# Attention ahead of two mixtures of experts: loading keys and queries by token instead of by token pair

## The chip, the cores and the metric

The kernel runs on one core of a Trainium2 chip. The metric is the device time of one execution in microseconds, the median of three runs. A profile of one further execution gives the trace that is read here. Engine names are those of the profile: PE (matrix products and transposes through the array), PEld (its weight loads), DVE (vector engine), ACT (scalar engine), POOL, and SP, whose queue issues most DMAs.

## What is computed

Block-local attention over 4 batches, 8 heads, 576 tokens and a head size of 64, then a mixture of experts with top-1 routing (8 experts, capacity 576), then a dense mixture with a Sinkhorn gate. The change touches the attention and the order of expert 0's loads only.

```
q_c, k_c, v_c = (a.reshape(B, H, nc, 64, D) for a in (q, k, v))
scores = scale * q_c @ k_c^T                 # within chunks of 64 tokens
attn = exp(scores - max); attn /= attn.sum(-1) + 1e-9
x = (attn @ v_c) -> [2304 tokens, 512]
x = moe(x, w_gate, w1, w2, capacity)         # top-1: relu(x @ w1[e]) @ w2[e], times the gate
out = moe2(x, w_gate, w1, w2)                # every expert, weights from 8 Sinkhorn rounds
```

## The kernel before

Attention goes over 18 tiles of 128 tokens (two chunks of 64), as a pipeline written out by hand. A loop over steps n runs the list `order`: each entry is a stage function and its lag, and stage f works on tile n minus lag. Every engine executes its share in exactly that order. A tile passes these stages: `st_tr` turns queries and keys on PE into a bank of PSUM and copies them out; `st_scores` multiplies them (per head pair, the keys as a block-diagonal matrix `kbd` of two heads); `st_max` (DVE) takes the maximum and subtracts; `st_dtr` turns the difference on PE; `st_exp` (ACT) writes eT; `st_pv` multiplies with `vbd`, a block-diagonal form of v; `st_x1` (DVE) normalises; `st_norm`, `st_scale`, `st_hi`, `st_lo` scale the row, split it into two half-precision parts and store it to `xs_d`; `st_xtr`, `st_xcopy` and `st_logits` turn x and multiply it with the first gate. Every three tiles `route` adds small DVE, PE and POOL work.

Keys and queries come in tiles of 256 tokens (`load_qk`, L433): a partition holds two consecutive tokens, so each packet of the DMA is 512 bytes. `st_tr` alternates: on an even step it turns the eight head pieces of a k tile, on an odd one the eight of a q tile. Since a turned piece holds two tokens on its 128 partitions, each of its two banks is copied out by two copies of 64 partitions, which put the tokens back in order (L458 for k, L461 for q): four half copies a step. For the first two 256-token tiles DVE does the copies of one bank; the rest are ACT's. The buffers are 2 for k, 4 for q, one for the copied q (`qT`), two for `kbd`. `load_v` (L443) issues four DMAs of 64 partitions a tile, 256-byte packets.

The turned pieces, the differences and x share three PSUM banks in turn (`in_turn("p", ...)`). Expert 0's weights are loaded, measured (`w_stat`, a sum of squares on ACT, L168), scaled and split (`w_split`: a high part on ACT, L239, a low part on DVE, L242) in quarters, at steps that the `plan` list fixes: the first matrix ("a") is loaded from step 4 on, the second ("b") from step 9. The steps from 18 on only drain the pipeline; at step 21 the first tokens of expert 0 are gathered and turned (`turn_into`), and `first_product` follows.

Of the kernel before, what the change touches and what calls it, by code (L numbers as in the profile page):

```python
# [11 lines left out]
F32 = mybir.dt.float32  # L12
# [18 lines left out]
def kernel(ctx, tc, q, k, v, w_gate, w1, w2, capacity, w2_gate, w21, w22, out):  # L31
    nc = tc.nc
    B, H, S, D = q.shape
    N, DM = out.shape
    E, _, F = w1.shape
    CH = 64
    NT = N // 128
    PR = H // 2
# [57 lines left out]
    ident = const.tile([128, 128], F32, name="ident")  # L96
# [204 lines left out]

    NS = N // 256
    runs = []
    for i in range(NS):
        r, done = [], 0
        while done < 256:
            b, s = divmod(i * 256 + done, S)
            n = min(256 - done, S - s)
            r.append((done // 2, n // 2, b, s))
            done += n  # L310
        runs.append(r)
# [57 lines left out]
    with ExitStack() as actx:  # L369
# [10 lines left out]
        nc.gpsimd.memset(warm, 0.0)  # L380
        kbd = [bd.tile([128, PR, 4, 128], F32, name=f"kbd{j}") for j in range(2)]
        for j in range(2):
# [42 lines left out]
        T = [dict() for _ in range(NT)]  # L425
        ST = [dict() for _ in range(NS)]
        GT = [dict() for _ in range(NG)]

        def load_qk(i):
            for nm, src in (("k", k), ("q", q)):  # L430
                t = io.tile([128, H, 2, D], F32, tag=nm, name=f"{nm}{i}", bufs=4 if nm == "q" else 2)
                for off, n, b, s in runs[i]:
                    nc.sync.dma_start(out=t[off:off + n].rearrange("p h t d -> p h (t d)"),  # L433
                                      in_=src[b, :, s:s + 2 * n, :].rearrange("h (s t) d -> s h (t d)", t=2))
                ST[i][nm] = t

# [8 lines left out]
        def st_tr(i):  # L445
            i, nm = i // 2, "kq"[i % 2]
            src = ST[i].pop(nm)
            t = ST[i][nm + "T"] = kbd[i % 2] if nm == "k" else at.tile([128, PR, 256], F32, tag="qT", name="qT", bufs=1)
            for h2 in range(2):
                p = in_turn("p", [128, PR, 128], F32, "p_t")  # L450
                for pr in range(PR):
                    nc.tensor.transpose(p[:, pr, :], src[:, 2 * pr + h2, :, :].rearrange("p t d -> p (t d)"), ident)
                hs = slice(64 * h2, 64 * h2 + 64)
                copy = nc.vector.tensor_copy if i < 2 and h2 == 0 else nc.scalar.copy
                for a in range(2):
                    pa = p[64 * a:64 * a + 64, :, :]
                    if nm == "k":
                        copy(out=t[hs, :, :, hs].rearrange("p r c (s t) -> p t r c s", t=2)[:, a],  # L458
                                       in_=pa.rearrange("p r (c s) -> p r c s", c=4))
                    else:  # L460
                        copy(out=t[hs].rearrange("p r (s t) -> p t r s", t=2)[:, a], in_=pa)  # L461

        def st_scores(i):
            qT, kT = ST[i // 2]["qT"], ST[i // 2]["kT"]
            p = ps_s.tile([128, PR, 128], F32, tag="s", name="p_s")
            for pr in range(PR):
                for c in range(2):
                    cc = 2 * (i % 2) + c
                    nc.tensor.matmul(p[64 * c:64 * c + 64, pr, :], lhsT=qT[:, pr, 64 * cc:64 * cc + 64],
                                     rhs=kT[:, pr, cc, :])  # L470
            T[i]["p"] = p.rearrange("p r (a s) -> p (r a) s", a=2)
# [77 lines left out]
        def st_xcopy(i):  # L549
            xT = T[i]["xT"] = at.tile([128, KD, 128], F32, tag="xT", name="xT")  # L550
            (nc.vector.tensor_copy if i % 3 == 1 or (i < 6 and i % 3 == 2) else nc.scalar.copy)(out=xT, in_=T[i].pop("xp"))

# [132 lines left out]

        load_qk(0)
        nc.scalar.activation(out=warm, in_=warm, func=AF.Exp)
        load_v(0)
        load_qk(1)
        nc.gpsimd.dma_start(out=g1, in_=w_gate.rearrange("(k p) e -> p k e", p=128))  # L690
# [14 lines left out]
        for h in range(2):  # L705
            plan(NT + 1, lambda h=h: w_load(1, "a", h))
        for nm, ld, st, sc, sp in (("a", 4, 6, 9, (11, 12, 13, 14)), ("b", 9, 11, 14, (18, 19, 20, 20))):
            for h in range(4):
# [883 lines left out]
```

## Time and profile before

| | us |
|---|---|
| median of 3 runs | 1741.5 (1738.76 to 1743.41) |
| profiled execution | 1743.53 |
| its span | 1741.8 |
| PE busy | 1691.9 |
| DVE busy | 1199.1 |
| ACT busy | 953.5 |
| POOL busy | 726.7 |

The span counts from the first to the last instruction of the profiled execution. A busy time is the sum over the instructions of an engine; for PE the ends of matrix products are modelled, so a busy PE isn't PE at its peak. The attention stage is the first 115 us or so of the span; the stretches and the order of time inside them tell more of it than the totals.

### The profile page before, as it was taken

The numbers are of one execution on the slowest core, as the hardware profiler recorded it, in microseconds if no ns is written. First come the engines' busy times: TensorE is split into PE (matmuls) and PEld (weight loads), VectorE is DVE, ScalarE is ACT, GpSimd is POOL, SyncE is SP. The second block draws the span as 40 slices with busy tenths as digits, with TensorE's granted clock in tenths as the row PEclk, the third lists the DMA queues.
The fourth block names the chain that finished last, engine by engine and source line by source line (L and its number), as shares of the span: only waits on it lengthen the run. The fifth ranks groups of instructions, "written<-read, shape, count | busy, mean of one in ns | idle before, by whom it ended". The sixth has DMA issues, their size and how long they took to land.

```text
span 1741.8 us, 33426 instructions
## 1 busy us (share of the span) xinstructions
PE 1691.9 (97%) x13203; PEld 1224.7 (70%) x13203; DVE 1199.1 (69%) x2336; ACT 953.5 (55%) x1805; POOL 726.7 (42%) x765
## 2 busy tenths in 40 slices
PE   8889999989999999999999999999999999999997
PEld 6775666655555577777777777777777767777776
DVE  7886857755578666776676767677766686677554
ACT  6976756754445554665455545455644665354431
POOL 2335644622023243553445434453534543453443
PEclk9999999999999999999999999999999999999999
DMA  9948878745242413242233224323323241323201
GB/s 227 248 142 243 228 182 195 198 113 143 82 155 94 144 53 134 65 176 85 92 129 131 87 98 148 107 86 113 130 89 133 65 174 47 131 66 126 91 34 49
DMA packets 140344, 219.17 MB, mean 126 GB/s; under 512 B 62304, under 2 KB 80832, under 8 KB 140160
## 3 DMA queue, kind: packets, MB, share of 16 engines
q1 hardware_dynamic: 134768, 199.46, 36.6%
q0 software_dynamic: 5392, 17.26, 3.6%
q8 instruction: 115, 1.88, 0.5%
q14 instruction: 69, 0.57, 0.2%
HBM read 167.56 MB, written 41.91 MB: 120 GB/s over the span
## 4 chain that ended last, share of the span: by engine, by line
PE 69%; DVE 5%; ACT 2%; issue 1%; POOL 1%; POOLq 0%; ACTq 0%; DVEq 0%
PE p_m L1283 36%; PE p_m L1379 28%; PE p_m L1427 5%; DVE wall L297 3%; DVE acc L1350 1%; ACT wall L296 1%; PE p_m L1171 0%; ACT eh L1288 0%; POOL out_dram L1361 0%; DVE el L1291 0%; ACT tq L1323 0%; DVE tq L1298 0%; POOL el L1295 0%; DVE tq L1301 0%; DVE wall L255 0%
## 5 line engine op out<-in xcount | busy, mean ns | idle before, releaser
L1283 PE MATMUL p_m<-x,wall 128*128 128x384 f16 x4032 | 667.7, 326 | 4.9 <-ACT tq L1323 4.1
L1295 POOL TENSOR_TENSOR el<-tq,eh 128x384 f16<-128x384 f32 x336 | 346.8, 1060 | 568.6 <-ACT eh L1288 567.9
L1379 PE MATMUL p_m<-wall,eh 128*128 128x256 f16 x3528 | 580.3, 273 | 0.0
L1283 PEld LDWEIGHTS <-wall 128*128 128x128 f16 x4032 | 394.3, 98 | 262.6 <-issue 8.3
L1379 PE MATMUL p_m<-wall,el 128*128 128x256 f16 x1764 | 480.8, 273 | 0.0
L1288 ACT ACTIVATE eh<-tq 128x384 f16<-128x384 f32 x540 | 274.1, 522 | 190.2 <-DVE tq L1301 101.4
L1379 PEld LDWEIGHTS <-eh 128*128 128x128 f16 x3528 | 344.3, 98 | 44.4
L1350 DVE SCALAR_TENSOR_TENSOR acc<-p_m,cf,acc 128x256 f32<-128x256 f32 (+1 forms) x378 | 175.6, 521 | 130.7 <-PE p_m L1379 130.7
L1298 DVE TENSOR_TENSOR tq<-p_m,tq 128x384 f32<-128x384 f32 x288 | 158.4, 556 | 127.9 <-PE p_m L1283 126.8
L1379 PEld LDWEIGHTS <-el 128*128 128x128 f16 x1764 | 172.6, 98 | 19.9
L1291 DVE SCALAR_TENSOR_TENSOR el<-tq,eh 128x384 f16<-128x384 f32 x204 | 175.2, 860 | 10.0 <-ACT eh L1288 8.6
L1301 DVE SCALAR_TENSOR_TENSOR tq<-tq 128x384 f32<-128x384 f32 x252 | 133.1, 553 | 2.8
L353 PEld LDWEIGHTS <-wall 128*128 128x128 f16 x1344 | 107.3, 98 | 19.3 <-issue 7.2
L1323 ACT COPY tq<-p_m 128x384 f32<-128x384 f32 x96 | 45.6, 475 | 112.4 <-PE p_m L1283 109.9
L1427 PE MATMUL p_m<-wall,eh 128*128 128x512 f16 x288 | 85.6, 379 | 0.0
L275 POOL TENSOR_TENSOR tq<-stb 128x256 f32<-128x256 f32 x56 | 48.9, 873 | 81.9 <-DVE wsumsq L184 59.0
L1336 ACT ACTIVATE tq<-tq 128x384 f32<-128x384 f32 x84 | 43.9, 522 | 69.9 <-DVE tq L1298 69.9
L353 PE MATMUL p_p<-xT,wall 128*128 128x256 f16 x672 | 75.6, 272 | 3.7 <-DMA rk_d<-rkt 1.5
L296 ACT ACTIVATE wall<-stb,wsb 128x256 f16<-128x256 f32 (+1 forms) x56 | 31.3, 606 | 87.0 <-DMA wb_d<-wall 61.5
L275 POOL TENSOR_TENSOR tq<-sta 128x256 f32<-128x256 f32 x56 | 45.0, 804 | 72.8 <-DVE wall L297 43.3
L247 POOL TENSOR_SCALAR stb<-stb,wsb 128x1024 f32<-128x1024 f32 x16 | 53.6, 3350 | 52.0 <-DVE tq L1298 45.1
L297 DVE SCALAR_TENSOR_TENSOR wall<-stb,wsb,wall 128x256 f16<-128x256 f32 (+1 forms) x56 | 38.1, 690 | 50.9 <-ACT wall L296 48.1
(283 smaller groups left out, 2115.5 us busy)
## 6 DMA issues: line engine op xcount, KB each, us to landing
x<-xt_d SPq DMA_DIRECT2D x147, 384.0 KB
wb_d<-wall SPq DMA_DIRECT2D x20, 896.0 KB
wall<-wb_d SPq DMA_DIRECT2D x20, 896.0 KB
sta<-in_moe_w_dram SPq DMA_DIRECT2D x32, 512.0 KB
stb<-in_moe_w_dram SPq DMA_DIRECT2D x32, 512.0 KB
sta<-in_moe_w_dram SPq DMA_DIRECT2D x16, 1024.0 KB
stb<-in_moe_w_dram SPq DMA_DIRECT2D x16, 1024.0 KB
xt_d<-x SPq DMA_DIRECT2D x21, 384.0 KB
```

The lines of the kernel that those rows point to most:

```text
L275: nc.gpsimd.tensor_tensor(out=at(o), in0=at(u), in1=at(v), op=op)
L297: nc.vector.scalar_tensor_tensor(out=o[:, cs, 1], in0=src, scalar=m.s, in1=o[:, cs, 0], op0=ALU.mult, op1=ALU.subtract)
L353: nc.tensor.matmul(p[:, f4, :], lhsT=w[:, kk, f * 128:(f + 1) * 128], rhs=xT[:, lo + kk, 0:W], start=(n == 0), stop=(n == 3 * KD - 1))
L1283: nc.tensor.matmul(p, lhsT=wt[:, w, lw, kk, :], rhs=xt[:, lx, kk, :], start=first and n == 0, stop=n == 5, skip_group_check=not first)
L1288: nc.scalar.activation(out=hs[op][0][:, q, :], in_=src, func=AF.Relu if op in (A11, A12, A22) or plain else AF.Copy)
L1291: nc.vector.scalar_tensor_tensor(out=hs[op][1][:, q, :], in0=src, scalar=0.0, in1=hs[op][0][:, q, :], op0=ALU.max, op1=ALU.subtract)
L1295: nc.gpsimd.tensor_tensor(out=hs[op][1][:, q, :], in0=src, in1=hs[op][0][:, q, :], op=ALU.subtract)
L1298: nc.vector.tensor_tensor(out=o, in0=a, in1=b, op=ALU.add)
L1301: nc.vector.scalar_tensor_tensor(out=o, in0=a, scalar=0.0, in1=b, op0=ALU.max, op1=op)
L1350: nc.vector.scalar_tensor_tensor(out=acc[:, j, cols], in0=y, scalar=coefs[x][:, j:j + 1], in1=acc[:, j, cols], op0=ALU.mult, op1=ALU.add)
L1379: nc.tensor.matmul(bk.t[:, cols], lhsT=hs[op][lh][:, q, t * 128:(t + 1) * 128], rhs=b.q[q][:, w, lw, :], start=m in (1, 5) and q == 0 and ...
L1427: nc.tensor.matmul(y.t, lhsT=h[:, kk % 4, c * 128:(c + 1) * 128], rhs=w[:, kk, :], start=(n == 0), stop=(n == 3 * KF - 1))
```

## The change

Keys and queries are now loaded in tiles of 128 tokens, one token a partition (`load_kq`), with 256-byte packets; both have five buffers. `st_tr` works on both of one tile in one step: four pieces of k into one bank, four of q into another. A turned piece holds two heads on its partitions, so k goes into `kbd` (half as large) by two copies of 64 partitions, and q is copied by one copy of 128 partitions. `st_tr` has lag 1 instead of 0 (of 256-token tiles). DVE copies k for the first three tiles, and `st_xcopy` leaves tiles 2 and 5 to ACT. The loads, sums and splits of expert 0's weights stand at later steps.

```
-        while done < 256:
-            b, s = divmod(i * 256 + done, S)
-            n = min(256 - done, S - s)
-            r.append((done // 2, n // 2, b, s))
+        while done < 128:
+            b, s = divmod(i * 128 + done, S)
+            n = min(128 - done, S - s)
+            r.append((done, n, b, s))
...
-        kbd = [bd.tile([128, PR, 4, 128], F32, name=f"kbd{j}") for j in range(2)]
+        kbd = [bd.tile([128, PR, 2, 128], F32, name=f"kbd{j}") for j in range(2)]
...
-        def load_qk(i):
+        def load_kq(i):
             for nm, src in (("k", k), ("q", q)):
-                t = io.tile([128, H, 2, D], F32, tag=nm, name=f"{nm}{i}", bufs=4 if nm == "q" else 2)
+                t = T[i][nm] = io.tile([128, H, D], F32, tag=nm, name=f"{nm}{i}", bufs=5)
                 for off, n, b, s in runs[i]:
-                    nc.sync.dma_start(out=t[off:off + n].rearrange("p h t d -> p h (t d)"),
-                                      in_=src[b, :, s:s + 2 * n, :].rearrange("h (s t) d -> s h (t d)", t=2))
+                    nc.sync.dma_start(out=t[off:off + n], in_=src[b, :, s:s + n, :].rearrange("h s d -> s h d"))
...
         def st_tr(i):
-            i, nm = i // 2, "kq"[i % 2]
-            src = ST[i].pop(nm)
...
-            for h2 in range(2):
-                p = in_turn("p", [128, PR, 128], F32, "p_t")
+            p = {}
+            for nm in "kq":
+                src = T[i].pop(nm)
+                p[nm] = in_turn("p", [128, PR, 128], F32, "p_t")
                 for pr in range(PR):
-                    nc.tensor.transpose(p[:, pr, :], src[:, 2 * pr + h2, :, :].rearrange("p t d -> p (t d)"), ident)
...
-                    if nm == "k":
-                        copy(out=t[hs, :, :, hs].rearrange("p r c (s t) -> p t r c s", t=2)[:, a],
-                                       in_=pa.rearrange("p r (c s) -> p r c s", c=4))
-                    else:
-                        copy(out=t[hs].rearrange("p r (s t) -> p t r s", t=2)[:, a], in_=pa)
+                    nc.tensor.transpose(p[nm][:, pr, :], src[:, 2 * pr:2 * pr + 2, :].rearrange("p a d -> p (a d)"), ident)
+            kT = T[i]["kT"] = kbd[i % 2]
+            for hs in (slice(0, 64), slice(64, 128)):
+                (nc.vector.tensor_copy if i < 3 else nc.scalar.copy)(
+                    out=kT[hs, :, :, hs], in_=p["k"][hs].rearrange("p r (c s) -> p r c s", c=2))
+            T[i]["qT"] = at.tile([128, PR, 128], F32, tag="qT", name="qT")
+            nc.scalar.copy(out=T[i]["qT"], in_=p["q"])
...
-            (nc.vector.tensor_copy if i % 3 == 1 or (i < 6 and i % 3 == 2) else nc.scalar.copy)(out=xT, in_=T[i].pop("xp"))
+            (nc.vector.tensor_copy if i % 3 == 1 else nc.scalar.copy)(out=xT, in_=T[i].pop("xp"))
...
-        for nm, ld, st, sc, sp in (("a", 4, 6, 9, (11, 12, 13, 14)), ("b", 9, 11, 14, (18, 19, 20, 20))):
+        for nm, ld, st, sc, sp in (("a", 5, 7, 10, (12, 13, 14, 15)), ("b", 12, 15, 18, (20, 20, 21, 21))):
...
-                 (st_max, 2), (st_xcopy, 4), (st_tr, 0), (st_pv, 3), (st_logits, 5), (st_dtr, 2))
+                 (st_max, 2), (st_xcopy, 4), (st_tr, 1), (st_pv, 3), (st_logits, 5), (st_dtr, 2))
...
-            if n % 2 == 1 and n // 2 + 2 < NS:
-                load_qk(n // 2 + 2)
+            if 0 < n < NT - 2:
+                load_kq(n + 2)
```

What moves on ACT in one step in the middle of the stage. Before, from an exponential to the sum over a weight chunk (eT is the exponential, row the high part, sq the squares, wsq the sum):

```order
L490 ACTIVATE eT<-p_t 128x512
L535 ACTIVATE row<-x_648,x1s 128x512
L516 ACTIVATE sq,ssq_794<-x_764 128x512
L461 COPY qT<-p_t 64x512 x4
L168 ACTIVATE wsq,wmxa<-sta_395 128x1024
```

And now:

```order
L481 ACTIVATE eT<-p_t 128x512
L526 ACTIVATE row<-x_562,x1s 128x512
L507 ACTIVATE sq,ssq_680<-x_645 128x512
L450 COPY kbd_132<-p_t 64x8x64 x2
L453 COPY qT<-p_t 128x512
L168 ACTIVATE wsq,wmxa<-sta_467 128x1024
```

Four half copies of one 256-token tile have become two half copies and a full one of one 128-token tile; the rest stands as it did.

The second place is the start on SP's queue. Before:

```order
L433 DMA k_184<-in_k_dram 128x8x128
L433 DMA q_186<-in_q_dram 128x8x128
L443 DMA vbd_135<-in_v_dram 64x4x64 x4
L433 DMA k_193<-in_k_dram 128x8x128
L433 DMA q_195<-in_q_dram 128x8x128
```

And now:

```order
L431 DMA k_184<-in_k_dram 128x8x64
L431 DMA q_186<-in_q_dram 128x8x64
L431 DMA k_189<-in_k_dram 128x8x64
L431 DMA q_191<-in_q_dram 128x8x64
L439 DMA vbd_135<-in_v_dram 64x4x64 x4
L431 DMA k_197<-in_k_dram 128x8x64
L431 DMA q_199<-in_q_dram 128x8x64
```

The first load of k and the first of q are half as large, and those of the second tile stand ahead of v. Each of the later steps has a k and a q load where every other step had one of each of twice the size.

The third place is ACT's drain, around the turning of expert 0's first tokens (L340 before, L339 now; L239 is the high part of a weight split). Before:

```order
L516 ACTIVATE sq,ssq_1826<-x_1800 128x512
L239 ACTIVATE wall<-stb_855,wsb 128x1024 x2
L535 ACTIVATE row<-x_1800,x1s 128x512
L516 ACTIVATE sq,ssq_1883<-x_1864 128x512
L551 COPY xT<-p_t 128x512
L340 COPY wall<-p_t 128x4x128 x2
```

And now:

```order
L507 ACTIVATE sq,ssq_1840<-x_1814 128x512
L239 ACTIVATE wall<-stb_1154,wsb 128x1024 x2
L526 ACTIVATE row<-x_1814,x1s 128x512
L507 ACTIVATE sq,ssq_1906<-x_1887 128x512
L542 COPY xT<-p_t 128x512
L239 ACTIVATE wall<-stb_1154,wsb 128x1024 x2
L339 COPY wall<-p_t 128x4x128 x2
```

Two more weight splits stand directly ahead of the copies of the turned tokens.

## Rows read from the trace of the kernel before

**Rows 1.** Stretches: us, busy time (instructions) of each engine, PE clock, DMA share, GB/s.
```profile
60.00:70.00 10.00, 9.13 (x111) 7.79 (x107) 9.26 (x34) 9.84 (x17) 4.96 (x5) 1.00 1.04 284
...
120.00:130.00 10.00, 7.34 (x74) 6.32 (x73) 9.59 (x33) 6.21 (x12) 3.70 (x3) 1.00 0.36 113
```
**Rows 2.** Order of time, PEld, tile 3's step; routing: start, us, instruction [idle before <-releaser].
```profile
24.18 0.85 PEld L469 LDWEIGHTS p_s<-kbd,qT 128*64 128x64 f32 x16 [0.17 <-issue]
...
25.60 0.90 PEld L452 LDWEIGHTS p_t<-ident,q 128*128 128x128 f32 x8
...
28.52 0.51 PEld L485 LDWEIGHTS p_t<-ident,d 128*128 128x128 f32 x4
...
29.35 0.85 PEld L469 LDWEIGHTS p_s<-kbd,qT 128*64 128x64 f32 x16 [0.33 <-ACT qT L461]
...
61.79 0.10 PEld L596 LDWEIGHTS <-tri 128*128 128x128 f16 x1
...
62.20 0.85 PEld L469 LDWEIGHTS p_s<-kbd,qT 128*64 128x64 f32 x16
```
**Rows 3.** Order of time, ACT, from one exponential to the next.
```profile
47.31 0.60 ACT L490 ACTIVATE eT<-p_t 128x512 f32<-128x512 f32 x1
...
47.80 0.71 ACT L535 ACTIVATE row<-x,x1s 128x512 f16<-128x512 f32 x1
...
48.42 0.62 ACT L516 ACTIVATE sq<-x 128x512 f16<-128x512 f32 x1
...
49.03 2.57 ACT L461 COPY qT<-p_t 64x512 f32<-64x512 f32 x4
...
51.63 1.06 ACT L168 ACTIVATE wsq<-sta 128x1024 bf16<-128x1024 f32 x1
...
52.80 0.60 ACT L490 ACTIVATE eT<-p_t 128x512 f32<-128x512 f32 x1
```
**Rows 4.** Groups, 0 to 100 us: busy, mean ns | idle before <- releasers.
```profile
L458 ACT COPY kbd<-p_t 64x512 f32<-64x512 f32 x32 | 20.4, 638 | 9.6 <-PE p_t L452 9.2
L461 ACT COPY qT<-p_t 64x512 f32<-64x512 f32 x32 | 20.3, 635 | 3.0 <-issue 1.8 <-PE p_t L452 0.8
L469 PE MATMUL p_s<-kbd,qT 128*64 128x128 f32 x256 | 19.1, 296 | 4.3 <-ACT qT L461 3.9 <-DVE qT L461 0.3
...
L551 ACT COPY xT<-p_t 128x512 f32<-128x512 f32 x7 | 4.0, 576 | 0.1
```
**Rows 5.** Order of time, PE: first turning, first scores, scores of tile 16.
```profile
5.21 1.94 PE L452 MATMUL p_t<-ident,k 128*128 128x128 f32 x8 [5.21 <-DMA k<-in_k_dram]
...
7.04 2.19 PE L452 MATMUL p_t<-ident,q 128*128 128x128 f32 x8
...
10.54 1.98 PE L469 MATMUL p_s<-kbd,qT 128*64 128x128 f32 x16 [1.30 <-ACT qT L461]
...
100.06 0.85 PEld L469 LDWEIGHTS p_s<-kbd,qT 128*64 128x64 f32 x16
```
**Rows 6.** DMA packets at 3 to 4.5 us (k, q), 16.5 to 18 (v), 30 to 32 (split k, q).
```profile
DMA packets 1025, 0.52 MB, mean 344 GB/s; under 512 B 16, under 2 KB 1025, under 8 KB 1025
...
DMA packets 1315, 0.32 MB, mean 212 GB/s; under 512 B 1312, under 2 KB 1315, under 8 KB 1315
...
DMA packets 825, 0.42 MB, mean 208 GB/s; under 512 B 28, under 2 KB 824, under 8 KB 824
```
**Rows 7.** Order of time, SP's queue: issues of one tile's v.
```profile
29.67 2.95 SPq L443 DMA_DIRECT2D vbd<-in_v_dram  x4
```
**Rows 8.** Order of time, ACT and DVE around expert 0's first tokens.
```profile
113.81 2.17 ACT L239 ACTIVATE wall<-stb,wsb 128x1024 f16<-128x1024 f32 x2
...
117.58 1.06 ACT L340 COPY wall<-p_t 128x512 f16<-128x512 f16 x2
...
119.02 2.48 DVE L242 SCALAR_TENSOR_TENSOR wall<-stb,wsb,wall 128x1024 f16<-128x1024 f32 x2
...
121.91 0.72 ACT L535 ACTIVATE row<-x,x1s 128x512 f16<-128x512 f32 x1 [3.26 <-DVE x1s L526]
```

More of the change, by code (lines that the diff above doesn't have):

```diff
@@ L298, in w_quad @@
                                            op0=ALU.mult, op1=ALU.subtract)
-    NS = N // 256
     runs = []
-    for i in range(NS):
+    for i in range(NT):
         r, done = [], 0
-        while done < 256:
-            b, s = divmod(i * 256 + done, S)
-            n = min(256 - done, S - s)
-            r.append((done // 2, n // 2, b, s))
+        while done < 128:
+            b, s = divmod(i * 128 + done, S)
+            n = min(128 - done, S - s)
+            r.append((done, n, b, s))
             done += n
@@ L425 @@
         T = [dict() for _ in range(NT)]
-        ST = [dict() for _ in range(NS)]
         GT = [dict() for _ in range(NG)]
-        def load_qk(i):
+        def load_kq(i):
             for nm, src in (("k", k), ("q", q)):
-                t = io.tile([128, H, 2, D], F32, tag=nm, name=f"{nm}{i}", bufs=4 if nm == "q" else 2)
+                t = T[i][nm] = io.tile([128, H, D], F32, tag=nm, name=f"{nm}{i}", bufs=5)
                 for off, n, b, s in runs[i]:
-                    nc.sync.dma_start(out=t[off:off + n].rearrange("p h t d -> p h (t d)"),
-                                      in_=src[b, :, s:s + 2 * n, :].rearrange("h (s t) d -> s h (t d)", t=2))
-                ST[i][nm] = t
+                    nc.sync.dma_start(out=t[off:off + n], in_=src[b, :, s:s + n, :].rearrange("h s d -> s h d"))
         def load_v(i):
@@ L445, in st_tr @@
         def st_tr(i):
-            i, nm = i // 2, "kq"[i % 2]
-            src = ST[i].pop(nm)
-            t = ST[i][nm + "T"] = kbd[i % 2] if nm == "k" else at.tile([128, PR, 256], F32, tag="qT", name="qT", bufs=1)
-            for h2 in range(2):
-                p = in_turn("p", [128, PR, 128], F32, "p_t")
-                for pr in range(PR):
-                    nc.tensor.transpose(p[:, pr, :], src[:, 2 * pr + h2, :, :].rearrange("p t d -> p (t d)"), ident)
[L453 to L456, printed above, removed]
-                    if nm == "k":
-                        copy(out=t[hs, :, :, hs].rearrange("p r c (s t) -> p t r c s", t=2)[:, a],
-                                       in_=pa.rearrange("p r (c s) -> p r c s", c=4))
-                    else:
-                        copy(out=t[hs].rearrange("p r (s t) -> p t r s", t=2)[:, a], in_=pa)
+            p = {}
+            for nm in "kq":
+                src = T[i].pop(nm)
+                p[nm] = in_turn("p", [128, PR, 128], F32, "p_t")
+                for pr in range(PR):
+                    nc.tensor.transpose(p[nm][:, pr, :], src[:, 2 * pr:2 * pr + 2, :].rearrange("p a d -> p (a d)"), ident)
[5 more added lines that the diff above has]
+            nc.scalar.copy(out=T[i]["qT"], in_=p["q"])
         def st_scores(i):
-            qT, kT = ST[i // 2]["qT"], ST[i // 2]["kT"]
+            qT, kT = T[i].pop("qT"), T[i].pop("kT")
             p = ps_s.tile([128, PR, 128], F32, tag="s", name="p_s")
@@ L467, in st_scores @@
                 for c in range(2):
-                    cc = 2 * (i % 2) + c
-                    nc.tensor.matmul(p[64 * c:64 * c + 64, pr, :], lhsT=qT[:, pr, 64 * cc:64 * cc + 64],
-                                     rhs=kT[:, pr, cc, :])
+                    cs = slice(64 * c, 64 * c + 64)
+                    nc.tensor.matmul(p[cs, pr, :], lhsT=qT[:, pr, cs], rhs=kT[:, pr, c, :])
             T[i]["p"] = p.rearrange("p r (a s) -> p (r a) s", a=2)
@@ L684, in route @@
                     [r_kx, r_acc, r_out])
-        load_qk(0)
+        load_kq(0)
         nc.scalar.activation(out=warm, in_=warm, func=AF.Exp)
+        load_kq(1)
         load_v(0)
-        load_qk(1)
+        load_kq(2)
         nc.gpsimd.dma_start(out=g1, in_=w_gate.rearrange("(k p) e -> p k e", p=128))
```

## The prediction

> **What bounds the kernel now.** I read the ten-microsecond stretches first. The diff touches only the attention stage, which fills the first 115 us; from 60 to 70 us ACT is busy for 9.84 of 10 us and PE for 9.13 [rows 1], so two engines are almost full. The order of time inside one step says which of them waits. PE's weight loads of the step of tile 3 start at 24.18 us with the scores and come back to the scores at 29.35 us [rows 2]. Everything between them is back to back; only the last 0.33 us is a wait, for ACT's copy of qT. PE's own work is therefore 28.52 + 0.50 - 24.18 = 4.84 us a step. The routing products of a group of three tiles take another 0.41 us (61.79 to 62.20 us [rows 2]), 0.14 a step; with the few other small products I allow 0.25, so PE's floor is 5.1 us.
>
> ACT's step goes from one exponential at 47.31 us to the next at 52.80 us [rows 3]: 0.49 exponential, 0.62 row, 0.61 squares, 2.60 for four half copies of qT, 1.17 for a sum over a weight chunk, 5.49 us in all and without a gap. An xT copy (0.58 us by its mean [rows 4]) comes on top where it is ACT's. From tile 3's scores at 24.18 us to tile 16's at 100.06 us [rows 2, 5] there are 13 steps in 75.9 us, 5.84 each. ACT's work in them, 13 x 4.32 + 6 xT copies x 0.58 + 12 weight operations x 1.17, is 73.7 us, 97% of it. So ACT paces the middle of the stage, and PE's scores stand 3.9 us waiting for its qT [rows 4].
>
> After the stage the order is fixed in the program and every later load is issued behind the earlier ones, so I let a gain at the end of attention pass on whole.
>
> **The change part by part.**
>
> ACT's copies. One tile's copies were four halves, 2.60 us. Now they are two halves of k at 0.638 and one full copy of q, for which the nearest row is the xT copy of the same shape at 0.576 [rows 4]: 1.85 us, 0.75 less. Two xT copies (tiles 2 and 5) come from DVE to ACT. In the same 13 steps ACT then has 13 x 3.57 + 8 x 0.58 + 11 x 1.17 = 63.9 us. That is below PE's 13 x 5.1 = 66.3, so PE becomes the later one. Its transposes cost the same: eight a step, four of k and four of q instead of eight of either. DVE loses those two xT copies and has six half copies of k in place of eight half copies, so it is a little lighter.
>
> The floor isn't reached on every step. In the step of rows 2, which has no weight work, PE still waits 0.33 us; for 12 steps I take 5.1 + 0.2 = 5.3 us. One step now holds both a split of expert 0's first weights and a sum over its second ones (before there were four): ACT has 3.57 + 0.58 + 2 x 1.17 = 6.5 us there, and I take that. The middle comes to 12 x 5.3 + 6.5 = 70.1 us instead of 75.9: **5.8 us gained**. Its bounds are 9.6 (PE's floor) and 0.9 (first rival).
>
> The start. k's first load lets PE begin at 5.21 us, q's at 7.04, and the first scores run at 10.54 us [rows 5]. The first loads are now half as large: at 212 to 344 GB/s (below) a 0.26 MB load takes 0.8 to 1.2 us where 0.52 MB took 1.5 to 1.8, so q arrives some 1.3 us sooner. PE turns four pieces of q instead of eight, half of 2.19 us or 1.1 less [rows 5], and one ACT copy follows instead of two halves, 0.6 less. DVE's two k copies run beside this. That is 2.6 to 3.0 us for the first scores. Part of it goes back: tile 1's scores now need k and q of their own, turned behind the scores of tile 0, where before its k and q were already there. I keep **2.2 us**, between 1.2 (q's arrival alone) and 3.0.
>
> The loads. k and q of one tile are 0.52 MB in 2048 packets of 256 bytes instead of 1024 of 512. The trace has no such load over 128 partitions, so I bound it. Whole 512-byte loads ran at 344 GB/s in 1.5 us; v's 256-byte packets into 64 partitions at 212; and 512-byte packets into 64 partitions (the halves of one load that crosses a batch) at 208 [rows 6]. Packet size made no difference between the last two, half the partitions did. So the new loads lie between 1.52 and 2.47 us a tile. By bytes, v takes 1.24 us a tile (0.262 MB at 212), a row's write 0.92 and a weight chunk 1.85 (0.262 and 0.524 MB at the 284 GB/s of 60 to 70 us [rows 1]). The k and q of tile 17 come behind 18 such pairs, 15 v, some 9 row writes and all 8 weight chunks. With the stream begun at 3.7 us (k's arrival at 5.21 less its 1.5), they land at 3.7 + 18 x 2.47 + 15 x 1.24 + 9 x 0.92 + 8 x 1.85 = 89.8 us at the slow bound, at 72.7 us at the fast one. PE wants them 1.4 us after tile 16's scores (25.60 less 24.18 [rows 2]), at 100.1 - 8.0 + 1.4 = 93.5 us. There are 3.7 us to spare, so I cost the loads at nothing on the path; that cover is what rivals two and three take away.
>
> [...]
>
> Expert 0's weights. The first ones load one step later, the second ones three. In the tail the four ACT splits of the second weights move from steps 18, 19, 20, 20 to 20, 20, 21, 21, so two splits (2.17 us [rows 8]) now stand ahead of ACT's copies of the gathered tokens at 117.58 us. Queued behind them is PE's first product of expert 0. DVE is busy 9.59 of 10 us from 120 to 130 us [rows 1]; ACT waits 3.26 us for it until 121.91 us, while DVE's own splits from 119.02 us don't depend on the moved ones [rows 8]. So most of the delay lies beside DVE's run. I take **0.8 us lost**, between 0 and 2.2.
>
> Sum: 2.2 + 5.8 - 0.8 = 7.2 us. The profiled execution took 1743.5 us with a span of 1741.8; the runs' median is 1741.5, so the two agree within 2 us and I take the gain from the median: **1734.3 us**.
>
> **The rivals.**
>
> First, ACT stays in the way: only even tiles' scores waited for a copy made in the step before, now every tile's do. The 3.9 us of waits [rows 4] would go, but nine odd tiles would get 0.33 us each: 0.9 us for the middle. 2.2 + 0.9 - 0.8 = 2.3, so 1739.2 us. For it speaks that PE's order leaves one step between turning and scores; against it, that ACT's copies end 0.75 us sooner, more than the 0.33.
>
> Second, a packet takes as long at 256 bytes as at 512: 1025 packets in 1.5 us [rows 6] are 23.4 ns for each of 16 engines, so a tile takes 3.05 us and tile 17's loads land at 100.3 us, 6.8 us late. 7.2 - 6.8 = 0.4, so 1741.1 us. [...] Rows 6 speak against it.
>
> Third, slower: the loads stop overlapping. SP's DMAs of attention carry a wait for the one eight places earlier, and the change needs six or seven DMAs a tile where five or six did. If v's four take their issue time of 2.95 us [rows 7] instead of 1.24, tile 17's loads land 15 x 1.71 = 25.7 us later, at 115.5 us, 22.0 us late: 1741.5 + 14.8 = 1756.3 us. It decides once a tile's loads (2.47 + 2.95 + 0.92 = 6.3 us) can't be fetched ahead of a 5.3 us step. Eight in flight hold more than one tile, which speaks against it.
>
> Fourth, PE's floor holds throughout: 9.6 + 2.2 = 11.8 us, 1729.7 us.
>
> **How the numbers follow.** My forecast has a chance of 0.46 (about 1731 to 1738 by its bounds), the first rival 0.16, the second 0.14, the third 0.13, the fourth 0.11. The range 1728 to 1746 holds all but the third and the far ends. About 0.3%, 5.2 us, is what a measurement of this kernel can tell from no change. Faster by more, under 1736.3 us, are the fourth, most of the forecast and a little of the first: 0.55. Slower, over 1746.7 us, is the third: 0.13. The rest, 0.32, lies within.
>
> **What would show it.** In the changed kernel's trace the first scores should run near 8 us, the scores of tiles 3 and 16 should be about 70 us apart with ACT's share in the middle nearer 90% than 98%, and PE's waits for qT should be under 4 us. PE waiting for k or q loads in steps 12 to 18 would show rival two or three; first scores later than 9.5 us, or steps still at 5.8 us with ACT at 98%, would make the sum wrong. If PE runs at the lower clock through expert 0's first product near 110 us, the tail was dearer than 0.8 us.

## The result and the profile after

The changed kernel took 1753.9 us (median of 20 runs, 1742.2 to 1761.6) against 1743.9 us for the kernel before in the same job (20 runs, 1738.8 to 1748.3): a ratio of 1.0054, 95% interval 1.0037 to 1.0072. It is slower, by about 10 us, where 7 us of gain were forecast. Its runs also lie twice as far apart, 19 us against 9.5. The profiled execution is its fastest, 1742.2 us with a span of 1740.4 us. It shows the attention stage well; the loss of the slower runs has to be looked for in other executions.

The start and the scores of tiles 3 and 16, in order of time (start, us, engine, instruction [idle before <-releaser]), answer to [rows 2, 5]:

```profile
4.14 1.09 PE L447 MATMUL p_t<-ident,k 128*128 128x128 f32 x4 [4.14 <-DMA k<-in_k_dram]
...
7.31 1.98 PE L461 MATMUL p_s<-kbd,qT 128*64 128x128 f32 x16 [0.68 <-ACT qT L453]
...
20.40 0.85 PEld L461 LDWEIGHTS p_s<-kbd,qT 128*64 128x64 f32 x16 [0.17 <-ACT qT L453]
...
98.30 0.74 PEld L461 LDWEIGHTS p_s<-kbd,qT 128*64 128x64 f32 x14
```

The first scores come at 7.31 us instead of 10.54, and tile 3 is 3.8 us earlier. The 13 steps to tile 16 then take 77.9 us instead of 75.9. ACT's own work is no longer why: the stretch from 60 to 70 us, which answers to [rows 1], has it busy for 8.19 us where it was 9.84 (columns as there).

```profile
60.00:70.00 10.00, 8.32 (x98) 7.38 (x99) 6.96 (x27) 8.19 (x18) 3.48 (x5) 1.00 0.80 196
120.00:130.00 10.00, 9.53 (x79) 7.72 (x77) 9.30 (x33) 6.21 (x12) 1.38 (x2) 0.81 0.36 117
```

ACT's groups from 24 to 98 us (busy, mean ns | idle before <- releasers), with [rows 4]:

```profile
L450 ACT COPY kbd<-p_t 64x512 f32<-64x512 f32 x24 | 13.9, 578 | 0.3
...
L453 ACT COPY qT<-p_t 128x512 f32<-128x512 f32 x13 | 7.6, 586 | 0.3
...
L168 ACT ACTIVATE wsq<-sta 128x1024 bf16<-128x1024 f32 x4 | 4.2, 1057 | 10.2 <-DMA sta<-in_moe_w_dram 10.2
```

A tile's copies are 2 x 0.578 + 0.586 = 1.74 us (1.85 forecast, 2.60 before). But ACT stops 10.2 us, in four waits, for sta, the first weights of expert 0; before, that wait was 0.4 us. SP's queue and what follows on ACT and PE, in order of time:

```profile
29.73 0.72 SPq L431 DMA_DIRECT2D k<-in_k_dram  x1
30.49 1.01 SPq L431 DMA_DIRECT2D q<-in_q_dram  x1
31.60 3.13 SPq L439 DMA_DIRECT2D vbd<-in_v_dram  x4
34.77 0.60 SPq L157 DMA_DIRECT2D sta<-in_moe_w_dram  x1
...
38.93 1.06 ACT L168 ACTIVATE wsq<-sta 128x1024 bf16<-128x1024 f32 x1 [4.43 <-DMA sta<-in_moe_w_dram]
...
40.09 0.57 ACT L481 ACTIVATE eT<-p_t 128x512 f32<-128x512 f32 x1
...
40.72 0.66 PE L447 MATMUL p_t<-ident,q 128*128 128x128 f32 x4 [2.83 <-ACT eT L481]
```

SP has no pause between its issues from 0.81 us on, and reaches sta's first load at 34.77 us, 0.3 us after ACT came to a stop for it (38.93 - 4.43 = 34.50). Its issues hold waits of their own: the four of v take 2.95 us in [rows 7], 4.18 us from 36.58 and 5.06 us from 42.60 us, and most of what SP waits for there is PE, which frees v's buffers (first 120 us; waited for: us in total, times, longest):

```profile
SPq L439 <- PE p_t L447: 7.1, 7, 2.1
SPq L439 <- PE p_s L461: 5.8, 3, 2.8
SPq L439 <- PE p_x L490: 4.6, 8, 0.9
```

So sta's loads stand in SP's queue behind loads that wait for PE, PE waits for ACT's exponential, and ACT for sta. From 40 to 50 us PE's granted clock then is 0.66 in the mean, and from 42 to 48 us it is 0.50.

Expert 0's first product (L352) starts at 118.60 us; before it was 118.70. So in this execution the attention stage as a whole gained nothing, and the first MoE that follows took the usual time: the second one's first product came at 381.8 us (381.4 before). Behind the milestone the first products of expert 0 run at a granted clock of 0.50, where it was 1.00 before. After, then before:

```profile
118.60 2.72 PE L352 MATMUL p_p<-wall 128*128 128x256 f16 x12 [0.18 <-ACT wall L339]
...
118.70 1.49 PE L353 MATMUL p_p<-wall 128*128 128x256 f16 x12
```

### The profile page after: what moved, and what is told of

Same layout as the page of the kernel before. It is cut to its first block, busy times and chain, and to the rows that moved or that the text cites. A ratio compares the mean times of both kernels' runs of the same rounds, so it can differ in the third digit from the quotient of the medians.

```text
span 1740.4 us, 33449 instructions
## 1 busy us (share of the span) xinstructions
PE 1693.4 (97%) x13203; PEld 1227.5 (71%) x13203; DVE 1193.8 (69%) x2332; ACT 940.7 (54%) x1791; POOL 725.6 (42%) x765
## 3 DMA queue, kind: packets, MB, share of 16 engines
q8 instruction: 112, 1.84, 0.4%
## 4 chain that ended last, share of the span: by engine, by line
PE 69%; DVE 5%; ACT 2%; issue 1%; POOL 1%; POOLq 0%; ACTq 0%; DVEq 0%
PE p_m L1275 36%; PE p_m L1371 28%; PE p_m L1419 5%; DVE wall L297 3%; DVE acc L1342 1%; ACT wall L296 1%; PE p_m L1163 0%; ACT eh L1280 0%; POOL out_dram L1353 0%; DVE el L1283 0%; ACT tq L1315 0%; POOL el L1287 0%; DVE tq L1290 0%; DVE tq L1293 0%; DVE wall L255 0%
## 5 line engine op out<-in xcount | busy, mean ns | idle before, releaser
L352 PEld LDWEIGHTS <-wall 128*128 128x128 f16 x1344 | 108.6, 99 | 20.6 <-issue 7.3
L352 PE MATMUL p_p<-xT,wall 128*128 128x256 f16 x672 | 75.6, 272 | 4.9 <-DMA xT<-xg 1.6
L168 ACT ACTIVATE wsq<-sta 128x1024 bf16<-128x1024 f32 x64 | 67.4, 1054 | 11.5 <-DMA sta<-in_moe_w_dram 10.2
```

The costliest lines, as they stand in the source:

```text
L168: nc.scalar.activation(out=sq, in_=src, func=AF.Square, accum_out=m.mx[:, h:h + 1])
L352: nc.tensor.matmul(p[:, f4, :], lhsT=w[:, kk, f * 128:(f + 1) * 128], rhs=xT[:, lo + kk, 0:W], start=(n == 0), stop=(n == 3 * KD - 1))
```

## The experiments

Three theories were set against each other. **A**: the loss is in the attention stage, in expert 0's new steps or in the loads. **S**, a form of A: SP's queue. **C**: the loss lies behind the stage. The same two milestones of each profile tell them apart: expert 0's first product ("attention ends", us from the start of the span) and the first product of the second MoE ("to p_m", us from the one milestone to the other). The time is a median of several executions; the milestones come from the one that was profiled. From p_m to the end of the span all 20 profiles take 1358.1 to 1360.9 us, so their differences lie ahead of it.

| kernel | time, us | ratio to before | attention ends | to p_m |
|---|---|---|---|---|
| before | 1743.9 | 1 | 118.7 | 262.7 |
| after (fastest run) | 1753.9 | 1.0054 | 118.6 | 263.2 |
| e1 (after again) | 1753.0 | 1.0046 | 118.9 | 271.6 |
| e2 sums later | 1751.0 | 1.0037 | 118.0 | 270.7 |
| e4 weights on POOL | 1748.8 | 1.0013 | 117.3 | 269.3 |
| e5 before, new steps | 1742.1 | 0.9986 | 116.6 | 262.4 |
| f1 before, 18 dead | 1755.9 | 1.0054 | 120.0 | 277.7 |
| f2 after, 238 dead | 1749.2 | 1.0018 | 123.8 | 265.2 |
| f3 after, early hints | 1751.1 | 1.0025 | 122.7 | 263.3 |
| f4 after, 128 dead | 1753.5 | 1.0042 | 124.7 | 268.7 |
| g1, h4 hints, half v on POOL | 1741.0, 1742.9 | 0.9961, 0.9969 | 116.7, 117.6 | 264.5, 262.5 |
| g2 hints, weights on POOL | 1746.3 | 0.9996 | 116.6 | 264.8 |
| g3 before, new steps, hints | 1744.9 | 0.9971 | 116.5 | 271.1 |
| g4 after, old steps, hints | 1754.2 | 1.0037 | 127.6 | 265.6 |
| h1 before, all three aids | 1740.4 | 0.9964 | 117.7 | 261.6 |
| h2 half v on POOL, no hints | 1748.1 | 0.9998 | 115.1 | 272.3 |
| h3 hints, all v on POOL | 1740.7 | 0.9953 | 114.3 | 266.9 |
| j1 hints, v on POOL from tile 3 | 1745.2 | 0.9988 | 115.1 | 265.7 |
| j2 before, same aids as j1 | 1745.8 | 0.9990 | 118.3 | 264.9 |

Only kernels of one letter ran in the same job; across letters the ratios are to be compared (the kernel before took 1743.9 to 1747.5 us). The intervals of the ratios are 0.0014 to 0.0024 to either side.

### Which part of the change: e1, e2, e4, e5

e1 is the changed kernel again. e2 moves expert 0's sums two steps later, e4 gives its weight loads to POOL, e5 is the kernel before with the new steps alone.

```diff
-(("a", 5, 7, 10, (12, 13, 14, 15)), ...
+(("a", 5, 9, 12, (14, 15, 16, 17)), ...            # e2
-        nc.sync.dma_start(out=m.st[:, h * c:(h + 1) * c, :],
+        (nc.gpsimd if x == 0 else nc.sync).dma_start(...   # e4
```

> The changed kernel once more, for a second trace. In its first trace ACT stands 10.2 us for expert 0's first weights (sta), four times, and PE behind it. Theory A (the loads come late because SP's queue is behind, and the two steps from load to sum are too few): a run of about 1754 us shows the same four waits, longer (15 us or more), and more time at the lower PE clock behind them. Theory B (the DMA engines are full, because packets are half as large): PE waits for k, q or v as well, over 3 us. Theory C (the loss lies behind the attention stage): attention ends as early as in the first trace, and a later stretch is longer.

> Only expert 0's first weights are used later: their sums from step 9 on instead of 7, their scales and splits two steps later too; loads as in the changed kernel. Theory A: ACT's wait for sta falls under 1 us, PE's stalls and the clock drop at 42 us go, and the time is 1736 to 1742 us (two more steps now hold two weight operations, about 2 us). Theory B: the waits move to PE's k, q and v, and the time stays above 1748 us. Theory C: no change, 1754 us.

> Expert 0's eight weight loads are issued by POOL instead of SP, everything else as in the changed kernel: the same bytes through the same DMA engines, but not behind SP's queue. Theory A: ACT's wait for sta under 1 us, time 1732 to 1738 us. Theory B: the same bytes still don't fit; waits for k, q, v or the weights stay, above 1748 us. Theory C: 1754 us.

> The kernel before with expert 0's loads, sums and splits at the changed kernel's steps, nothing else. Theory A: SP's queue is shorter there (five loads a tile instead of six), so the weights come in time; 1741 to 1746 us, at most 1 us of ACT waiting for sta. If the later steps are themselves the cause (theory D): 1750 us or more.

e5 was, if anything, faster than before (0.9986, 0.9972 to 1.0001): expert 0's steps aren't the loss. In e1 ACT waited 10.5 us for sta, as in the first profile and not the 15 us or more that theory A asked for. e2 and e4 took ACT's wait for sta away, yet PE then waited for v (4.5 to 5.0 us in e2, 3.4 us in e4), and both took longer than theory A gave: most of the loss stayed in e2 (1.0037), a part of it in e4 (1.0013, 0.9995 to 1.0031). The profile of e1, 10 us slower than that of after, says where it is: not in the stage, which ended within 0.3 us, but in front of the first product of a later expert block. Order of time of PE, e1 first, then the same place in after:

```profile
273.25 0.38 PE L888 MATMUL p_y<-w,hl 128*128 128x512 f16 x1
280.42 0.80 PE L352 MATMUL p_p<-xT,wall 128*128 128x256 f16 x3 [6.79 <-PEq L1055]
```
```profile
273.44 0.38 PE L888 MATMUL p_y<-w,hl 128*128 128x512 f16 x1
274.37 0.81 PE L352 MATMUL p_p<-xT,wall 128*128 128x256 f16 x6 [0.55 <-DMA rk_d<-rkt]
```

PEq is PE's sequencer, and L1055 the conditional `with tc.If(rc > 384, ...)`, which here jumps over a block of 128 tokens that isn't needed. Its branch instructions in the same stretch (ns, min/median/max of the two), e1 and after:

```profile
L1055 PEldq COMPARE_BRANCH  x2: 191/5064/9938, 269.9 to 280.1; - x2
```
```profile
L1055 PEldq COMPARE_BRANCH  x2: 196/1010/1824, 270.1 to 274.0; - x2
```

One took 9.9 us, the other 1.8. TensorE's code arrives by DMA (the page of after has 112 packets and 1.84 MB in a queue of its own, 16 KB each; from 400 to 1700 us 75 of them stand against 19216 products and weight loads of TensorE, 256 to a piece). By the packets' records one such piece starts at 269.5 us in after and 269.9 us in e1, the next at 276.6 and 276.5 us. In after the branch ends 1.4 us after the first has landed, in e1 1.4 us after the second. Between them lie the weight loads of the stretch, which land 8.8 us (after) and 11.7 us (e1) after their issue. It is the same everywhere: of the 60 branches of TensorE that took more than 1.5 us in the 20 profiles, 59 ended 1.2 to 1.6 us after a piece of code had landed. In e1, PE stands idle from 273.6 us, the granted clock is 0.60 in the mean from 276 to 278 us, and behind the wait PE runs at a granted clock of 0.50:

```profile
280.00:282.00 2.00, 1.58 (x8) 1.15 (x9) 0.00 (x0) 0.00 (x0) 0.00 (x0) 0.50 1.04 197
```

### The place of the code: f1, f2, f4, and the hints: f3

The change adds 18 instructions to TensorE's program (29560 rows instead of 29542, by the count in f1's expectation; the trace shows 17 of them running, all of them waits and all in the attention stage), so everything behind the stage stands 18 places further on. The experiment adds TensorE instructions that never run, in a block of expert 0 that is skipped, and leaves all else as it is.

```diff
                     with tc.If(rc > 512, label=f"o{x}"):
                         rest()
+                        if x == 0:
+                            p = in_turn("c", [128, 128], F32, "p_pad")
+                            turns["c"].insert(0, turns["c"].pop())
+                            for _ in range(9):    # f1; 119 in f2, 64 in f4
+                                nc.tensor.matmul(p[:, 0:1], lhsT=id16, rhs=id16[:, 0:1], start=True, stop=True)
```

f3 moves the hint on which way a branch will go (`skip`) ahead of the block's products:

```diff
-                    further(2, [[lambda: skip("n")], [], []])
+                    skip("n")
+                    further(2, [[], [], []])
...
-                    further(3, [[lambda: skip("o")], [], []])
+                    skip("o")
+                    further(3, [[], [], []])
```

> The kernel before with 18 TensorE instructions (9 weight loads and 9 one-column products) added to a block of the first expert that is skipped in every run. Nothing that runs is different; all TensorE code behind the block stands 18 instructions further on, as it does in the changed kernel (29560 rows against 29542). Theory C (the loss lies in the first MoE, at the conditional branches at which TensorE waits for its code, and the place of the code decides how often such a wait becomes 6 to 10 us long): the time rises to about that of the changed kernel, 1749 to 1756 us, and the branch that ends expert blocks near 270 or 355 us takes 6 us or more in its profile. Rival A (the loss is in the attention stage: loads and expert 0's steps): within 0.2% of the kernel before in the same job, about 1744 to 1746 us, branches of 2 to 4 us.

> The changed kernel with 238 TensorE instructions in the same skipped block, so that the code behind it stands 256 instructions further on than in the kernel before; 256 instructions of 64 bytes are one of the 16 KB pieces in which the profile shows TensorE's code arriving. Theory C: the waits of 6 us and more at the branches go away, and the time falls to what the first stage left it with, 1740 to 1746 us, some 8 us below the changed kernel. Rival A: it stays at 1751 to 1755 us.

> The changed kernel with the hint for a branch ahead of the block of 128 tokens in front of it, in place of behind the first group of its products; some 5 us earlier in TensorE's stream, so about 10 us ahead of the branch in place of 5.2. Theory C, if what matters is that the hinted code has landed when the branch comes: the waits at the last two kinds of branch fall below 1 us and the time falls to 1738 to 1745 us. Theory C, if it's the place of the code alone: no change, 1750 to 1755 us. Rival A: no change, 1751 to 1755 us.

> The changed kernel with 128 TensorE instructions in the skipped block: the code behind it is half a 16 KB piece further on. Theory C: another place, so another set of long branches; somewhere between 1740 and 1758 us, and not equal to both of the two other places within 2 us. Rival A: 1751 to 1755 us, as the changed kernel.

f1 shows that the place of the code is enough: 18 instructions that never run make the kernel before as slow as the changed one, 1.0054 (1.0031 to 1.0077). The same branch in f1, near 273 and near 365 us:

```profile
L1063 PEldq COMPARE_BRANCH  x2: 196/4530/8864, 273.4 to 282.5; - x2
...
L1063 PEldq COMPARE_BRANCH  x2: 201/3150/6100, 365.5 to 371.8; - x2
```

In both, the branch ends 1.3 us after a second piece of code has landed, as in e1. The block that f1 makes longer belongs to expert 0; the long branches are those of later experts, whose code only stands further on.

The other way round, f2 puts the changed kernel's code where the kernel before had it, but for 256 instructions, one 16 KB piece, and this branch is short again; near 277 us:

```profile
L1055 PEldq COMPARE_BRANCH  x2: 186/1345/2504, 277.2 to 281.1; - x2
```

Another branch grew in its place, the one behind a block of 256 tokens at 313 to 329 us, and it shows best that the place decides which branch waits. Before, f2 and after:

```profile
L1060 PEldq COMPARE_BRANCH  x1: 4182/4182/4182, 316.4 to 316.4; - x1
...
L1052 PEldq COMPARE_BRANCH  x1: 5433/5433/5433, 322.5 to 322.5; - x1
...
L1052 PEldq COMPARE_BRANCH  x1: 438/438/438, 315.4 to 315.4; - x1
```

All six kernels with the old place, to within one instruction (before, e5, f2, g3, h1, j2), take 3.2 to 5.7 us there, all fourteen with another place 0.4 to 0.5 us. Early or late ends of attention don't explain it: f2's stage ended at 123.8 us, h2's, with a branch of 10.0 us below, at 115.1.

f2's ratio is 1.0018 (0.9998 to 1.0038), where the changed kernel had 1.0046 and 1.0054; the intervals overlap a little, so the rows say more here than the times. Half a piece (f4) left a branch of 9.5 us and 1.0042, a time that both theories allowed. Early hints (f3) brought the branch to 2.2 us and the ratio to 1.0025 (1.0011 to 1.0039). Neither f2 nor f3 fell below 1746 us as theory C had it, and the reason stands in the table: in f2, f3 and f4 the attention stage itself ended at 122.7 to 124.7 us, 4 to 6 us later than before. So theory A holds a part too. ACT waited 11.7 to 13.6 us for sta in these three, and PE's granted clock from 25 to 95 us was 0.88 to 0.90 in the mean (0.95 in after, 1.00 before). Their code for the stage is that of after and e1, where the stage ended at 118.6 and 118.9 us; why it took longer in this job is open.

### SP's queue: g1 to g4

All four have the early hints, with which the branch of e1 and f1 took 2.2 us in f3.

```diff
-                    nc.sync.dma_start(out=t[64 * h2:...], in_=src[h2])
+                    (nc.sync if h2 == 0 else nc.gpsimd).dma_start(out=t[64 * h2:...], in_=src[h2])   # g1
```

> The changed kernel with the early hints of f3_after_hints_early, and with half of v's loads (two of a tile's four) issued by POOL in place of SP. Theory S (in the attention stage SP's queue is the limit: the changed kernel issues 112 loads of k, q and v where the kernel before issues 96, each some 0.6 us of SP, so expert 0's first weights land late and ACT waits 10 to 13 us for them): ACT's waits for sta fall below 4 us in all, the first product of expert 0 (L352) starts at 114 to 118 us and not at 118.6 to 123, and the time is 1740 to 1746 us, 5 us or more below f3_after_hints_early against the same kernel before (ratio 0.996 to 1.000). Rival D (the 16 DMA engines are the limit, since the packets of k and q are half as long and twice as many): the waits move to the tiles of v, k and q, and the ratio stays at 1.002 to 1.004.

> The changed kernel with the early hints, and with expert 0's eight weight loads issued by POOL (e4_weights_on_pool with the hints). Theory C (code position and branches behind the attention stage): 3 to 6 us below e4's ratio of 1.0013, so 0.998 to 1.000, 1741 to 1746 us; no branch over 3.5 us in the profile. If the branches were a side effect and not the cause: 1.001 to 1.002 as in e4.

> The kernel before with two things: the changed kernel's steps for expert 0 (as e5_before_new_steps, 0.9986) and the early hints. Its branches took 0.9 to 5 us in the profiles. Theory C: the branch of 4 to 5 us behind the block of 256 goes unchanged (its hint is not moved), the others lose 1 us each, ratio 0.996 to 0.999, 1736 to 1742 us. If early hints cost something of their own: 1.000 or more.

> The changed kernel with the early hints and with expert 0's loads, sums, scales and splits at the steps of the kernel before. Theory S and rival D: the weights come one step earlier in SP's queue and ACT waits less for them (under 6 us), but k, q and v come later, so the ratio stays between 1.001 and 1.005. If the later steps were what cost the attention stage its gain: 0.997 to 1.000.

g1, with half of v's loads on POOL, is faster than the kernel before, 0.9961 (0.9937 to 0.9985), against 1.0025 for f3. ACT's wait for sta fell to 7.2 us (under 4 was expected) and the stage ended at 116.7 us. g2 came to 0.9996, a gain on e4 that its interval doesn't separate from none. g3 gave 0.9971 as expected, though its profile has a branch of 5.7 us behind a block of 256, whose hint wasn't moved, and its 271.1 us to p_m are more than that branch explains. g4, with the old steps, came to 1.0037 as expected, but ACT's wait for sta, expected under 6 us, was 11.8, and attention ended last of all, at 127.6 us: the later steps help the changed kernel.

### What is left of the change: h1 to h4, j1, j2

h1 and j2 are the kernel before with the new steps, the hints and v on POOL as in h4 and j1; h4 is g1 again.

> The kernel before with expert 0's new steps, the early hints and half of v's loads on POOL, that is, all that g1_half_v_on_pool has but the new loading of k and q. If the new loading is worth the 5 to 8 us that the prediction gave it once SP and the branches are out of the way: 5 us or more above h4_half_v_again. If it's worth only its earlier start: 2 to 3 us above. If it's worth nothing: within 1.5 us of it, 1739 to 1742 us.

> The changed kernel with half of v's loads on POOL and the hints where they were. If the two causes add up: 3 to 6 us above h4_half_v_again, ratio 0.999 to 1.001, with a branch of 6 us or more in some executions. If SP's queue was the cause of both (the branch waits being only a matter of when the stage ends): within 1.5 us of h4_half_v_again.

> As g1_half_v_on_pool, with all four of v's loads of a tile issued by POOL. Theory S: SP issues 40 loads and the weights in the stage, ACT's waits for sta go below 2 us (7.2 in g1), and the time is that of h4_half_v_again or up to 3 us less, unless POOL, whose wait for p_x before each load was 24.6 us in g1, holds up its own scatter of rows; then 2 to 6 us more. Rival D (the DMA engines): ACT's waits stay at 5 us or more and the time stays within 1 us.

> The same kernel as g1_half_v_on_pool, beside the three others: ratio 0.994 to 0.9985 as there, 1738 to 1743 us.

> The changed kernel with the early hints, and v's loads issued by POOL from tile 3 on (tiles 0 to 2 by SP as before). If SP's queue was what took the gain: the start of f2 and f3 (first scores at 7.1, tile 3 at 20.2 to 20.8) and then 13 steps of 70 to 72 us, first product of expert 0 at 112 to 115 us, and 2 to 5 us below j2. If the new loading is worth nothing even then: within 1.5 us of j2. Ratio to the kernel before 0.992 to 0.996.

> The kernel before with expert 0's new steps, the early hints and v's loads issued by POOL from tile 3 on. If ACT is its bound there (97% busy in the middle of the kernel before): 13 steps from tile 3 to tile 16 of 74 to 76 us, the same time as h1_before_all_aids, ratio 0.995 to 0.9985. If SP held it up too: 1 to 3 us less than that.

The two causes add up: h2 without the hints is 5.2 us above h4, and its branch takes 10.0 us, although its stage ended early, at 115.1 us. And SP's queue is a cause in the stage. Issues of sta's four loads (ns, min/median/max, first and last start), before, after, h4 and h3:

```profile
L157 SPq DMA_DIRECT2D sta<-in_moe_w_dram x4: 334/610/627, 26.2 to 45.1; - x4
```
```profile
L157 SPq DMA_DIRECT2D sta<-in_moe_w_dram x4: 602/602/618, 34.8 to 54.2; - x4
```
```profile
L157 SPq DMA_DIRECT2D sta<-in_moe_w_dram x4: 593/594/594, 32.8 to 51.0; - x4
```
```profile
L157 SPq DMA_DIRECT2D sta<-in_moe_w_dram x4: 3247/4040/4902, 23.3 to 41.4; - x4
```

ACT waits for them 0.4, 10.2, 5.4 and 0 us between 20 and 97 us. With no wait left, h3's 13 steps from tile 3 to tile 16 are these:

```profile
22.92 0.85 PEld L461 LDWEIGHTS p_s<-kbd,qT 128*64 128x64 f32 x16 [0.17 <-issue]
...
93.74 0.85 PEld L461 LDWEIGHTS p_s<-kbd,qT 128*64 128x64 f32 x16
```

That is 70.8 us; 70.1 were predicted. But h3 has all of v on POOL from the start and reaches tile 3 at 22.92 us, 2.5 us later than after. j1, which keeps the early start, missed its 70 to 72 us, and j2, the kernel before with the same aids, its 74 to 76; j1 first:

```profile
20.32 0.85 PEld L461 LDWEIGHTS p_s<-kbd,qT 128*64 128x64 f32 x16 [0.17 <-ACT qT L453]
...
94.75 0.85 PEld L461 LDWEIGHTS p_s<-kbd,qT 128*64 128x64 f32 x16
```
```profile
24.17 0.42 PEld L469 LDWEIGHTS p_s<-kbd,qT 128*64 128x64 f32 x8 [0.17 <-issue]
...
97.03 0.85 PEld L469 LDWEIGHTS p_s<-kbd,qT 128*64 128x64 f32 x16 [0.40 <-ACT qT L461]
```

j1 took 74.4 us, with 4.1 us of ACT's wait for sta left, and j2 72.9; e5, the kernel before with the new steps alone, took 73.2 (23.31 to 96.54). So of the shorter middle 2.7 us come from the new steps, without the new loading, and at tile 16 the new loading is ahead of j2 by 2.3 us in j1 and 3.3 in h3. Rival D, the DMA engines as the limit, falls: h3 moves the same packets, from 25 to 95 us at 243 GB/s in the mean where after moved 225, and nobody waits for the weights; PE still waited 1.4 us for v between 20 and 97 us, which this doesn't settle. With v's loads on POOL, where they waited 5.0 us for PE in the same stretch, sta's first load is issued at 23.3 us instead of 34.8; that it is their waiting more than SP's 0.6 us for each that held sta up is my reading, no run separates the two.

Yet little of it reaches the end. h4 against h1 and j1 against j2 differ in the loading, turning and copying of k and q alone; h4 is 2.5 us slower than h1 (none of the cases in h1's expectation) and j1 0.6 us faster than j2, with 4 to 5 us of uncertainty to either side by the intervals. A gain of 5 us or more for the changed loading is not shown anywhere. j1's stage ended 3.2 us earlier than j2's; what became of that I can't say, since the MoE behind it varies by more from one execution to the next (263.2 us to p_m in after, 271.6 in e1, the same kernel). j1 also didn't repeat h3's 0.9953 (0.9937 to 0.9968): 0.9988 (0.9970 to 1.0007), on another chip, with a spread of 10 us. The best versions of the h job are h3 and h1, about 7 us under the kernel before in that job (0.9953, and 0.9964 with 0.9949 to 0.9979) and 0.3 us apart; only h3 has the changed loading.

## Why the prediction was wrong

**The start** was right in kind and too small: 3.2 us by the first scores, 3.8 by tile 3, where 2.2 were forecast. The part held back for tile 1's scores wasn't needed in full.

**ACT's copies** were right: 1.74 us a tile where 1.85 was forecast, and ACT's share from 60 to 70 us fell from 98 to 82%. PE's waits for the copies of qT and kbd fell to 1.5 us in all, so the first rival is wrong.

**The loads** are the first step that failed: "I cost the loads at nothing on the path". The sum there asked when tile 17's k and q land, 60 us away and with 3.7 us to spare. It didn't ask about the loads in the same queue that have a due time of their own: sta's four, whose first moved from 26.2 to 34.8 us, while the sums that want them moved by one step and the tiles came 3 to 4 us earlier. With the new steps alone (e5) it stands at 31.7 us and ACT waits 0.4 us; the other 3 us come with the new loading. The third rival came nearest, with SP's issue and its threshold (a tile's loads against a 5.3 us step: from 34.77 to 40.80 us SP took 6.0 us for one tile and a weight), but it looked for the victim among k and q, and took v's issue time for a price of issuing where part of it is a wait for PE. PE waited 0.3 us for q behind the start and never again for k, not 22 us, so that this rival's 1756.3 us lies near the measured 1753.9 is luck. The middle lost 2.0 us instead of gaining 5.8. h3, where the wait is gone, comes to 70.8 us for it, but from a later start, and j1 to 74.4 with the early one; the 70.1 behind an early start is not shown.

The second rival, a 256-byte packet as slow as one of 512, is wrong. From 2.5 to 4.5 us, with k and q of the first tiles alone, after moved:

```profile
DMA packets 2015, 0.51 MB, mean 254 GB/s; under 512 B 2015, under 2 KB 2015, under 8 KB 2015
```

So a tile's k and q take 0.524 MB / 254 = 2.06 us (2.17 by the 242 GB/s of 3 to 5 us), between the bounds of 1.52 and 2.47 and well under that rival's 3.05. The smaller packets were the slower ones all the same: 254 GB/s here, 344 in [rows 6] for 512 bytes. It didn't decide.

**The tail** was to lose 0.8 us. From the last scores to expert 0's first product took 12.1 us before and 14.3 after, a loss of 2.2, the far end of its bounds. The new steps alone, with the old loading, make the same loss: e5's tail took 14.5 us. The two moved splits do stand ahead of the copies as forecast:

```profile
115.42 2.19 ACT L239 ACTIVATE wall<-stb,wsb 128x1024 f16<-128x1024 f32 x2
117.50 1.05 ACT L339 COPY wall<-p_t 128x512 f16<-128x512 f16 x2
```

The prediction's last sign came true too: the first 12 products of expert 0 ran at a granted clock of 0.50, 2.72 us against 1.49 before.

In the profiled execution the sum is thus -3.8 + 2.0 - 0.5 (tile 17's step) + 2.2 = -0.1 us, as measured.

**That a gain passes on whole** is the second step that failed, and the dearer one: "after the stage the order is fixed in the program". The order is, the time isn't. The first MoE took 261.6 to 277.7 us between the same two milestones; in all seven profiles over 268 us a branch of 5.7 to 10.0 us stands in it, in the other thirteen none over 5.4 (g3, where 5.7 us don't explain the 271.1, is the weakest case). The 18 instructions added in the attention stage moved the code of all later ones. f1 alone has a loss as large as the measured 0.5%, without any other part of the change; in f2 to f4 the stage's own loss of 4 to 6 us comes beside it. How the two share the 10 us differs by execution, and I can't give one split.

Left open: why 18 places turn a hinted branch of 2 us into one of 9 in many executions and not in all, and which instruction's place decides. The packet records show which piece it waits for, not what the sequencer had asked for.

## To carry to other kernels

Before calling a load free, list every load of the same queue with its due time, and see which has the least to spare; here the four loads of a tile's v took 3.13, 4.18 and 5.06 us of SP's queue (from 31.60, 36.58 and 42.60 us), waits for PE included, and sta's between them are the ones that ACT waited 10.2 us for. In a program with branches at run time compare several executions, look for waits on the sequencer, and test with instructions that never run before crediting or blaming the edit: with 18 such instructions (f1) a later branch took 8.9 us in the profile, where it took 2.3 before. In the changed kernel, hints given one block of products earlier (h2 to h4, 5.2 us) and v's issue spread over two queues (f3 to g1, 1.0025 to 0.9961) were each worth more than the changed loading was shown to be; in the kernel before, g3 and h1 (0.9971 and 0.9964) show no further gain from the second.

## What the runs showed of the hardware

The same compare-and-branch took 0.1 to 10.0 us on TensorE, whose code arrived in pieces of 16 KB in a DMA queue of its own, 112 of them in after; after a wait of 6.8 us the granted clock was 0.50. One that took more than 1.5 us ended 1.2 to 1.6 us after a piece of code had landed, in 59 of 60 cases. Loads of 256-byte packets over all 128 partitions ran at 242 to 254 GB/s, those of 512 bytes at 344 [rows 6]; over 64 partitions the two had 212 and 208 [rows 6]. In these windows the packet's size made a difference only over all 128. SP's issue of one load took 0.3 to 0.6 us in three of four cases of the first 120 us, before and after; sta's four in h3, issued far ahead of their use, took 3.2 to 4.9 us each and nobody waited for them.
